# One new order for all the steps of a fused recurrence and MLP kernel

## The chip, the cores and the metric

The kernel runs on one core of a Trainium2 chip. A core has five engines that each work through a queue of their own in order: PE (TensorE, matrix products), DVE (VectorE), ACT (ScalarE), POOL (GpSimd) and SP (SyncE, which here only issues DMA transfers). An engine waits for another by a semaphore: the first instruction that needs a result stops its whole queue until the result is there. The metric is the time of one execution in microseconds (us).

## The reference

Two blocks follow each other. The first is a recurrence over 768 time steps, for 4 batches with 8 heads each, with a state of 40 by 40 numbers per head:

```python
    for t in range(S):
        kt, vt, rt = (k[:, :, t], v[:, :, t], r[:, :, t])
        wt, at, bt = (w[:, :, t], a[:, :, t], b[:, :, t])
        y[:, :, t] = np.einsum('bhd,bhde->bhe', rt, state)
        Sa = np.einsum('bhde,bhe->bhd', state, at)
        state_decay = state * wt[:, :, None, :] - np.einsum('bhd,bhe->bhde', Sa, bt)
        state = state_decay + np.einsum('bhd,bhe->bhde', vt, kt)
```

Its result, put together over heads to 3072 rows of 320, goes through an MLP: `h = x @ w_in` (320 to 2048), the exact GELU, and `g @ w_out` (2048 to 320). The inputs of the recurrence are float32, the two weights come as float64, and the result is float32.

## The kernel before

**Tiling.** Time is cut into 12 chunks of 64 steps. Inside a chunk the recurrence is written as matrix products with masks; it needs the inverse of a triangular matrix for each batch and head. Between chunks the 40 by 40 states are handed on. The MLP of a chunk starts when the chunk's y is there. So three things run side by side: the preparation of a chunk from its inputs, which needs no state; the part that hangs on the state; and the MLP of the chunk before.

**The steps.** Each piece of work is a small function, a step, and carries the number of its chunk: `mh.3.6` is the step mh of chunk 3 with argument 6. Those that matter here, in the order in which one chunk meets them:

- `tw`, `lt`, `pw`, `ew`, `en` (DVE and ACT): logarithms of the decays, their running sum (`pw`, line 717) and two exponentials. `ta`, `tb`, `tk`, `tv`, `tr` turn the inputs (DVE transposes), `sa`, `sn`, `kc`, `sb`, `sk` scale them.
- `nm` (PE) makes the triangular matrices, `nk` (DVE) masks them, `nd` (ACT) copies a part, `nx` (DVE, line 925) writes them into the tile Nb as POOL wants them. There is one Nb.
- `iz` and `ic` (POOL, line 955): the inversion, 31 steps of a product into tmp and a sum into W. Each needs the one before it.
- `wx` (DVE, line 931) takes W out into Tt, `tc_` (DVE, line 1066) transposes it, `jm` (PE, line 1070), `jc`, `km`, `kt0`, `kt1` put the inverses of the blocks together; `wa` and `wb` are copies by ACT for the same end.
- `am`, `vm`, `av`, `ym`, `xm`, `sm`, `pk`, `pb`, `cu` are products of PE for the chunk, with `ak`, `vk`, `sc`, `xc0`, `xc1`, `yc` as what DVE and ACT do to their results. `oa`, `od` (DVE), `oc`, `ot` (ACT, lines 1267 and 1271) and `tn` (DVE) make the next state; `om` and the transfers `ox` make the MLP's input.
- `mh.c.0` to `mh.c.7` (PE, line 1302): the first MLP product, in tiles of 64 by 128, two at a time; `ge` (ACT) is the GELU. The second product is done with seven smaller ones, `m1` to `m7` (PE), on sums `s1` to `s4` (DVE), and put together by `e1`, `e3` (ACT copies out of PSUM) and `e2`, `e4`, `e5`, `e6` (DVE sums). `so` and `sz` store the output.
- Steps with an L in front load; `ce`, `cs`, `cm`, `cv`, `cl`, `cn`, `cg` turn the weights from 64 bit to 32 bit at the start. `warm` steps are products without use that keep PE busy at the start.

**What sets the order.** All engines are scheduled by hand: one long list of step names, the function `order`, is performed from its first name to its last, and every engine's queue holds its instructions in that order. Waits follow from it. A step that reads a tile which an earlier step in the list writes waits for it, and a step that overwrites a tile waits for earlier readers.

**PSUM.** Products land in four banks of PSUM, which the steps borrow and give back (`take` and `drop`, from line 176). A bank can hold two results: `m5` and `m6` share one, `take`n by `m5` for two readers, `e3` and `e4`.

```python
    def product(c, name, n, l_, r_):
        po = bank(f"{name}{c}") if n else take(f"{name}{c}", 2 if name == "m56_" else 1)
        for f in range(NF // 2):
            nc.tensor.matmul(po[:, n, :DM // 2], l_[:, f], r_[:, f], start=f == 0, stop=f == NF // 2 - 1)
    def e3(c):
        nc.scalar.copy(c22, result(c, "m56_", 0))
        drop(f"m56_{c}")
```

Of the kernel before, what the change touches and what calls it, by code (L numbers as in the profile page):

```python
# [18 lines left out]
def order(chunks, first_seven):  # L19
    return """  # L20
        first_ones.1 Lw.1 stripes_set identity pads_extra.1 sums_mask Lw.0 pads_r.1 warm.4.20 upper_mask
        pads_extra.3 La.0 pads_a.1 warm.4.0 pads_VR.1 pads_VR.0 of_half_set Lb.0 bias_set warm.4.13 pads_r.0 lg.1
        first_ones.0 pads_w.0 pads_rows.0 warm.4.25 pads_extra.0 Lb.1 pads_rows.1 onward_set lg.0 pads_w.1 wT.1
        pads_a.0 pads_extra.2 La.1 wT.0 warm.4.2 ew.1 Lf.0.1.0 ta.0 Lf.1.1.0 cu.0 Lf.0.0.0 cu.1 ec.0 Lf.1.0.0
        ew.0 sb.0 tb.0 sa.0 Lk.0 warm.4.15 sn.0 ec.1 nm.0 sb.1 Lf.2.0.0 warm_set tb.1 nk.0 Lf5.0.0 ta.1 sn.1 qt
        parity_set iz.1 sa.1 qm.0 qi.0.p qi.1.v nm.1 qz.0 warm_first ce.1 Lf.3.0.0 nk.1 qb.0.0.v Lf.3.1.0 qc.0
        cs.1 qb.0.1.a nd.1 qm.1 sk.0.p ce.0 nx.1 Lr.0 cm.1 Tt_zero tk.0 cs.0 cn.1 ic.1.0.4 qc.1 Lf.2.1.0 cl.1
        cx.1 qz.1 kc.0 Lf5.0.1 qb.1.0.v qa.1 qb.1.1.a cm.0 cy.1 ic.1.4.8 qm.2 Lf.0.0.1 cv.0 ce.3 LV.0 warm.4.18
        qz.2 am.0 qb.2.0.v qa.2 cs.3 ic.1.8.12 tr.0 Lf.1.0.1 ce.2 ak.0 Lw.2 qb.2.1.a cs.2 qc.2 Lf.0.1.1 rc.0 qm.3
        Lk.1 ic.1.12.16 Lf.2.0.1 qa.3 qz.3 Lf5.1.1 tv.0 qb.3.0.v qb.3.1.a cm.3 cm.2 cv.3 qm.4 vc.0 ic.1.16.20  # L30
        vm.0 qa.4 ql warm.4.4 vk.0 lg.2 Lf.2.1.1 ce.5 cv.2 av.0 Lf.3.1.1 ic.1.20.24 qc.3 qx jm.0 sk.1.v warm.4.24
        cs.5 Lf.1.1.1 cm.5 cv.5 Lf5.1.0 jc.0 km.0 xc0.0 xc1.0 ic.1.24.28 ce.7 Ls.3 cu.2 kt1.0 Ls.4 cs.7 kt0.0
        cm.7 sm.0 ic.1.28.31 cv.7 LV.1 ec.2 pk.0 sc.0.0 Lr.1 ce.9 sc.0.1 tk.1 cs.9 Lb.2 pb.0 kc.1 cm.9 cv.9 ce.4
        La.2 tv.1 om.0.1 om.0.0 Ls.2 cs.4 cm.4 Lf.3.0.1 vc.1 tr.1 od.0.1 cv.4 ox.0.0 am.1 rc.1 unused.v wT.2 ce.6
        sb.2 warm.4.1 one_set od.0.0 wx.1 ew.2 ta.2 ox.0.1 tb.2 sa.2 vm.1 sn.2 cs.6 cl.6 cm.6 nm.2 vk.1 oc.0 cn.6
        mh.0.0 nk.2 ot.0.1 cg.6 ot.0.0 ak.1 Ls.1 nd.2 Ls.0 nx.2 mh.0.1 iz.2 ce.8 tn.0 LV.2 unused.a mh.0.2 wb.1
        cs.8 ic.2.0.4 Lk.2 cm.8 cv.8 ge.0.0 av.1 Ls.6 ce.11 ym.1 ce.10 cs.11 ic.2.4.8 Ls.5 mh.0.3 tc_.1 Lr.2
        cm.11 yc.1 sk.2.v xm.1 cs.10 Ls.7 ge.0.1 cm.10 tv.2 ic.2.8.12 Ls.9 xc1.1 cv.10 xc0.1 Ls.10 jm.1 vc.2
        cv.11 Ls.8 tr.2 ce.12 tk.2 Ls.11 mh.0.6 ce.13 cs.12 ic.2.12.16 La.3 cm.12 kc.2 cs.13 mh.0.7 wa.1.1 cm.13
        jc.1 cv.12 rc.2 am.2 vm.2 cv.13 ic.2.16.20 ce.14 pm.0.0 Ls.13 cl.14 cs.14 Ls.12 ce.15 cm.14 ak.2 Lw.3  # L40
        cn.14 cs.15 km.1 wa.1.0 cg.14 vk.2 pm.0.1 kt1.1 ta.3 kt0.1 Ls.15 cm.15 Ls.14 cv.15 ic.2.20.24 ce.16 Lbt.3
        sm.1 ge.0.3 cs.16 ce.17 mh.0.4 sc.1.0 Lwt.3 sc.1.1 cl.17 ic.2.24.28 cm.16 mh.0.5 cs.17 Lr.3 cm.17 lg.3
        cv.16 pk.1 cn.17 cg.17 pb.1 ge.0.2 oa.1.0 cu.3 Lk.3 oa.1.1 pm.0.3 ec.3 od.1.0 Lw.4 ic.2.28.31 od.1.1 oc.1
        tw.3 ot.1.0 om.1.1 sk.3.p ot.1.1 om.1.0 av.2 tn.1 ox.1.1 pc.0.1 lt.3 ym.2 wx.2 iz.3 pm.0.2 tc_.2 yc.2
        unused.r pw.3 so.0.1 ew.3 tb.3 ox.1.0 jm.2 wb.2 en.3 pc.0.0 xm.2 jc.2 sn.3 km.2 xc0.2 tr.3 mh.1.0 xc1.2
        La.4 sa.3 wa.2.1 kt1.2 wa.2.0 nm.3 kt0.2 so.0.0 sm.2 nk.3 Lkt.3 mh.1.1 nd.3 sc.2.0 nx.3 lg.4 Lv.3 pk.2
        sc.2.1 ic.3.0.4 pb.2 ge.1.0 tk.3 mh.1.6 ic.3.4.8 oa.2.0 Lr.4 ta.4 mh.1.7 ws.0 LV.3 ws.1 mh.1.4 ge.1.3
        Lbt.4 ic.3.8.12 tr.4 mh.1.5 oa.2.1 Lk.4 kc.3 mh.1.2 tv.3 od.2.0 Lwt.4 ic.3.12.16 mh.1.3 od.2.1 oc.2
        om.2.0 vm.3 Lb.3 ge.1.1 am.3 ge.1.2 vk.3 m1.1 ot.2.1 ic.3.16.20 s1.1 ot.2.0 om.2.1 m2.1 s2.1 ox.2.1 ak.3
        m5.1 e1.1 tn.2 ws.3 av.3 e3.1 ic.3.20.24 s3.1 Lkt.4 ym.3 e2.1 tw.4 m6.1 yc.3 s4.1 ox.2.0 m3.1 ws.2 lt.4  # L50
        tk.4 m7.1 ic.3.24.28 e4.1 LV.4 tb.4 m4.1 e5.1 Lr.5 ic.3.28.31 xm.3 e6.1 pw.4 so.1.1 mh.2.6 xc0.3 La.5
        wx.3 ew.4 tc_.3 cu.4 sb.3 jm.3 en.4 so.1.0 mh.2.7 wb.3 sn.4 Lv.4 wa.3.0 jc.3 xc1.3 wa.3.1 km.3 sa.4 ec.4
# [1414 lines left out]
```

## Time and profile before

| | |
|---|---|
| time, median of 3 runs | 637.75 us (637.71 to 638.87) |
| span of the profiled execution, first to last instruction | 638.6 us |
| PE busy | 621.4 us, 97% |
| DVE busy | 457.9 us, 72% |
| POOL busy | 380.3 us, 60% |
| ACT busy | 323.6 us, 51% |
| DMA, mean | 100 GB/s |

The profile gives the busy time of each engine, groups of equal instructions by source line (count, busy us, mean ns of one, and the idle time just ahead of them with what ended it), the waits, and the chain of work that ended last. The profiled execution's own time is not listed apart from its span; the span lies within the range of the three runs and 0.85 us above their median. Times in a timeline count from the span's start. A row of the windows gives the stretch, its length, then for PE, its weight loads (PEld), DVE, ACT and POOL the busy us and the number of instructions, then the granted clock of PE as a share of the full one, the share of DMA and its GB/s.

### The profile page before, as it was taken

To read this page: it belongs to the slowest core of one execution; us is meant where nothing else is said; L and a number is where in the kernel's file an instruction comes from. 1 tells how busy PE (TensorE), PEld (TensorE's weight loads), DVE (VectorE), ACT (ScalarE), POOL (GpSimd) and SP (SyncE) were. 2 spreads that over 40 slices of the span, in tenths; PEclk is the share of its full clock that TensorE was granted. 3 is DMA by queue.
4 is the path that set the end of the run, shared out by engine and by line. 5 is a ranking of instruction groups with operands and counts; after the bars stand their busy time and mean duration, and the time that the engine had idled before them with its cause. 6 is when DMAs were issued, how large, how long until landed. Compare 5 with 4: busy or idle time off the path is not lost.

```text
span 638.6 us, 27896 instructions
## 1 busy us (share of the span) xinstructions
PE 621.4 (97%) x12418; PEld 548.3 (86%) x12418; DVE 457.9 (72%) x557; ACT 323.6 (51%) x456; POOL 380.3 (60%) x782
## 2 busy tenths in 40 slices
...
GB/s 136 181 162 178 91 178 187 143 104 137 91 135 149 59 98 159 64 147 111 110 84 133 76 93 107 88 88 157 68 92 109 41 37 84 42 26 3 36 7 21
DMA packets 246899, 64.07 MB, mean 100 GB/s; under 512 B 228380, under 2 KB 243644, under 8 KB 246780
## 3 DMA queue, kind: packets, MB, share of 16 engines
...
## 4 chain that ended last, share of the span: by engine, by line
PE 76%; ACT 2%; DVE 0%; issue 0%; DVEq 0%
PE bank L1307 30%; PE bank L1346 27%; PE bank L193 19%; ACT Tt L937 0%; ACT SM L1154 0%; ACT L1312 0%; ACT spare L922 0%; DVE spare L864 0%; ACT st L1194 0%; ACT gt L1312 0%; ACT T L942 0%; DVE Tt L932 0%; ACT st L1192 0%; ACT Tt L1116 0%; DVE os L1299 0%
## 5 line engine op out<-in xcount | busy, mean ns | idle before, releaser
L1307 PE MATMUL bank<-xt,w_in_sb 64*128 64x256 f32 x1920 | 221.3, 381 | 0.2 <-ACT gt L1312 0.2
L961 POOL TENSOR_TENSOR tmp<-W,Nb 128x126 f32<-128x126 f32 (+22 forms) x341 | 164.4, 482 | 93.1 <-DVE Nb L927 67.6
L1307 PEld LDWEIGHTS bank<-xt,w_in_sb 64*128 64x128 f32 x1920 | 182.5, 187 | 25.1 <-issue 1.5
L963 POOL TENSOR_TENSOR W<-W,tmp 128x126 f32<-128x126 f32 (+22 forms) x341 | 168.8, 495 | 26.7
L1346 PE MATMUL bank<-w_out_sb,gt 128*128 128x160 f32 x704 | 101.1, 301 | 0.0
L1346 PEld LDWEIGHTS bank<-w_out_sb,gt 128*128 128x128 f32 x704 | 96.6, 190 | 2.2 <-issue 1.2
L1312 ACT ACTIVATE gt<-bank 128x1024 f32<-128x1024 f32 x48 | 48.7, 1024 | 94.9 <-PE bank L1307 94.6
L1175 DVE TENSOR_TENSOR SM<-bank,upper 128x832 f32<-128x832 f32 (+1 forms) x24 | 23.0, 988 | 20.3 <-PE bank L193 20.2
L1263 ACT COPY conv<-st 32x128 f32<-32x128 f32 (+2 forms) x55 | 28.0, 509 | 17.0 <-DVE st L1257 16.2
L1299 DVE TENSOR_TENSOR conv<-gt 128x1024 f32<-128x1024 f32 x11 | 14.2, 1290 | 25.1 <-ACT gt L1312 25.0
L1227 DVE TENSOR_TENSOR st<-bank,st 128x832 f32<-128x832 f32 (+1 forms) x22 | 21.2, 985 | 14.0 <-PE bank L193 14.0
L1346 PE MATMUL bank<-extra,conv 128*128 128x160 f32 x208 | 30.3, 300 | 0.0
L1299 DVE TENSOR_TENSOR os<-os,bank 128x160 f32<-128x160 f32 x44 | 13.8, 315 | 22.1 <-PE bank L1346 20.5
L1346 PEld LDWEIGHTS bank<-extra,conv 128*128 128x128 f32 x208 | 28.9, 190 | 0.1
L721 DVE TENSOR_TENSOR_SCAN kT<-spare,kT 128x256 f32<-128x256 f32 x36 | 26.6, 798 | 0.6 <-ACT kT L714 0.6
L1346 PE MATMUL bank<-extra,gt 128*128 128x160 f32 x176 | 25.8, 300 | 0.0
L1346 PEld LDWEIGHTS bank<-extra,gt 128*128 128x128 f32 x176 | 24.5, 190 | 0.1
L789 POOL TENSOR_TENSOR bk_rows<-bk_rows,part 128x640 f32<-128x640 f32 x9 | 14.3, 1591 | 14.3 <-ACT part L742 13.9
L1312 ACT ACT_TABLE_LOAD x17 | 21.8, 1283 | 0.3
L1346 PE MATMUL bank<-extra,SM 128*128 128x160 f32 x144 | 21.2, 300 | 0.0
L193 PEld LDWEIGHTS bank<-SM,Tt 64*64 64x64 f32 x768 | 17.1, 133 | 4.2 <-issue 2.3
L193 PE MATMUL bank<-SM,Tt 64*64 64x104 f32 (+1 forms) x768 | 19.3, 249 | 0.9 <-ACT Tt L1113 0.9
...
## 6 DMA issues: line engine op xcount, KB each, us to landing
...
```

The lines of the kernel that those rows point to most:

```text
L193: nc.tensor.matmul(o, lhsT, rhs, start=first, stop=True, skip_group_check=True)
L721: nc.vector.tensor_tensor_scan(logs[:, at:at + n], onward, logs[:, at:at + n], 0.0, ALU.mult, ALU.add)
L789: (nc.vector if q == "v" else nc.gpsimd).tensor_tensor(to, rows(k_of(c)), decays(c), ALU.mult)
L961: nc.gpsimd.tensor_tensor(t, W[:, BL // 2 - rows:, rest:rest + 1].to_broadcast([P, rows, rest]), Nb[:, rest:rest + 1, :rest].to_broadcast( ...
L963: nc.gpsimd.tensor_tensor(own, own, t, ALU.add)
L1175: nc.vector.tensor_tensor(SM[:, g, :, :, cols], pair_of(f"S{c}_", g).rearrange("p x i c -> p i x c")[:, :, :, cols], kept, ALU.mult)
L1227: nc.vector.tensor_tensor(to, pair_of(f"QY{c}_", g)[:, :, :, cols], to, ALU.add)
L1263: nc.scalar.copy(apart.rearrange("p e i g d -> p (e i g) d")[to_rows, :, to_col:to_col + n], st.rearrange("p e i g c -> p (e i g) c")[rows ...
L1299: nc.vector.tensor_tensor(to, one_, other, how)
L1307: nc.tensor.matmul(ph[:, x, s], w_in_sb[half(x), kt, p * P:(p + 1) * P], xt[half(x), kt], start=kt == 0, stop=kt == NK - 1)
L1312: nc.scalar.activation(gt[:, 4 * q:4 * q + 4].rearrange("p (x s) t -> p x s t", x=2), bank(f"ph{c}_{q}").rearrange("p x (s t) -> p x s t", ...
L1346: nc.tensor.matmul(po[:, n, :DM // 2], l_[:, f], r_[:, f], start=f == 0, stop=f == NF // 2 - 1)
```

## The change

The list in `order` is replaced by another list of the same 1450 steps. Every step is performed once, as before, with the same arguments; the functions are the same. The first MLP product stays in tiles of 64 by 128. What differs is the place of nearly every step, from the first memset to the last sums, so every engine's queue and SP's queue of transfers are in a new order, banks of PSUM are lent in a new order, and waits that follow from who comes first in the list are different ones. Below is the core of the diff: the two places from chunk 3 to chunk 5, and those around e3.6 and e3.9.

```diff
 def order(chunks, first_seven):
     return """
...
-        tk.4 m7.1 ic.3.24.28 e4.1 LV.4 tb.4 m4.1 e5.1 Lr.5 ic.3.28.31 xm.3 e6.1 pw.4 so.1.1 mh.2.6 xc0.3 La.5
-        wx.3 ew.4 tc_.3 cu.4 sb.3 jm.3 en.4 so.1.0 mh.2.7 wb.3 sn.4 Lv.4 wa.3.0 jc.3 xc1.3 wa.3.1 km.3 sa.4 ec.4
...
-        ak.4 pw.5 m3.2 e3.2 ew.5 m7.2 La.6 e2.2 ic.4.20.24 tn.3 en.5 e4.2 m4.2 e5.2 av.4 e6.2 tk.5 so.2.1
-        ic.4.24.28 ym.4 sn.5 Lr.6 mh.3.6 yc.4 sa.5 tv.5 LV.5 xm.4 ic.4.28.31 cu.5 xc1.4 xc0.4 mh.3.7 ec.5 wx.4
-        tc_.4 wa.4.1 iz.5 ta.6 nm.5 ge.3.3 vm.5 Lbt.6 tr.6 wb.4 jm.4 nk.5 mh.3.2 jc.4 nd.5 Lwt.6 wa.4.0 nx.5
...
-        s4.6 m5.6 so.5.0 oa.7.0 od.7.0 LV.9 om.7.0 m1.6 oa.7.1 ic.8.20.24 om.7.1 m2.6 s2.6 ox.7.1 od.7.1 ew.9
-        m6.6 s3.6 en.9 tr.9 ec.8 m3.6 e1.6 ic.8.24.28 oc.7 e2.6 sa.9 Lkt.9 e3.6 ot.7.0 m7.6 e4.6 ot.7.1 sn.9
...
-        ic.11.20.24 s3.9 m6.9 kc.11 od.10.0 m3.9 Lb.11 e3.9 e2.9 e4.9 ox.10.0 m7.9 ic.11.24.28 am.11 e5.9 vm.11
...
+        ta.4 m5.1 so.0.1 e3.1 s4.1 yc.3 ox.2.0 m6.1 ox.2.1 xm.3 xc0.3 xc1.3 e2.1 e4.1 m3.1 m7.1 wx.3 wa.3.0 m4.1 Lbt.4
+        tc_.3 jm.3 mh.2.4 Lv.4 wa.3.1 e5.1 mh.2.5 e6.1 lt.4 pw.4 Lkt.4 tb.4 mh.2.6 ew.4 so.1.1 sa.4 wb.3 en.4 mh.2.7
+        sn.4 jc.3 ge.2.2 km.3 tk.4 Lr.5 La.5 tv.4 nm.4 Lwt.5 ge.2.3 kt1.3 kt0.3 LV.4 nk.4 cu.4 Lw.5 nd.4 kc.4 so.1.0
+        sk.3.p iz.4 nx.4 ic.4.0.4 ic.4.4.8 ic.4.8.12 ic.4.12.16 sm.3 sc.3.1 mh.2.2 mh.2.3 sc.3.0 sb.3 ic.4.16.20
...
+        yc.4 lg.5 wx.4 wa.4.0 mh.3.6 tc_.4 jm.4 jc.4 tb.5 sn.5 xm.4 sb.4 tv.5 mh.3.7 so.2.1 ge.3.3 mh.3.2 xc1.4 Lkt.5
+        Lb.5 xc0.4 sa.5 nm.5 tk.5 cu.5 sk.4.p nk.5 kc.5 vm.5 Lwt.6 wa.4.1 wb.4 km.4 mh.3.3 ec.5 kt1.4 kt0.4 sm.4 vk.5
...
+        pk.7 pb.7 s2.6 oa.7.1 oa.7.0 LV.9 od.7.1 ec.8 od.7.0 om.7.0 oc.7 ot.7.0 ot.7.1 so.5.0 ic.8.20.24 ic.8.24.28
+        ic.8.28.31 om.7.1 ew.9 m1.6 m2.6 s3.6 Lv.9 Lb.8 tb.9 tn.7 ox.7.1 en.9 sn.9 sa.9 m5.6 e3.6 Lw.9 e1.6 e2.6 m6.6
...
+        e1.9 am.11 ak.11 ic.11.0.4 ic.11.4.8 ic.11.8.12 ic.11.12.16 s4.9 vk.11 od.10.1 oc.10 ot.10.1 ot.10.0 m5.9 e3.9
...
     """.split()
```

At the start the first transfers, too, are in a new order: before, Lw.1, Lw.0, La.0, Lb.0, Lb.1, La.1 and then the weights (Lf); after, Lw.0, Lw.1, Lb.0, La.0, Lb.1, then two steps of weights, and La.1 behind them.

More of the change, by code (lines that the diff above doesn't have):

```diff
@@ L20, in order @@
     return """
[L21 to L50, printed above, removed]
```

127 lines of the change are left out of this document (76 added, 51 removed).

## The prediction

> **What bounds the kernel now.** I read the page first, then the busy times by stretch, the waits, the chain that ended last, and the timeline of single engines.
>
> ```profile
> span 638.6 us, 27896 instructions
> PE 621.4 (97%) x12418; PEld 548.3 (86%) x12418; DVE 457.9 (72%) x557; ACT 323.6 (51%) x456; POOL 380.3 (60%) x782
> ```
>
> ```profile
> 120.00:140.00 20.00, 17.12 (x406) 12.89 (x400) 15.08 (x21) 16.94 (x24) 7.49 (x12) 1.00 0.46 89
> ```
>
> PE is busy for 621.4 of 638.6 us. What it loses, 17.2 us, lies almost wholly in the first 140 us; the stretch shown, with 2.9 us of it, is the last that loses much. From there the chain that ended last is PE behind PE. So no order can gain more than some 17 us, but one that makes PE wait loses each microsecond of it. The question is whether PE, in its new order, ever reaches a step before its input is there. The candidates are the loops that leave PE and come back. Four pieces of the chain give PE's prices:
>
> ```profile
> 184.46 2.36 PE bank L1307 x20
> 202.98 3.01 PE bank L193 x128
> 210.51 2.02 PE bank L193 x128
> 212.54 15.41 PE bank L1346 x112
> ```
>
> That is, in order: one mh 2.36, pk with pb 3.01 (1.5 each, and I take the same for xm, which has as many products), am with vm 2.02 (1.0 each, nm too), the seven products m1 to m7 15.41 (2.2 each).
>
> The loop with least room is POOL's. Each chunk's 31 inversion steps (ic, L961 and L963) are one serial run, and the next chunk's run can start only when DVE has made its Nb (nx, L927).
>
> ```profile
> 184.01 0.51 POOL L963 TENSOR_TENSOR W<-W,tmp 128x16 f32<-128x16 f32 x1
> 199.13 0.24 POOL L961 TENSOR_TENSOR tmp<-W,Nb 128x31 f32<-128x31 f32 x1 [4.83 <-DVE Nb L927]
> 234.92 0.23 POOL L963 TENSOR_TENSOR W<-W,tmp 128x16 f32<-128x16 f32 x1
> 243.13 1.06 POOL L961 TENSOR_TENSOR tmp<-W,Nb 128x31 f32<-128x31 f32 x1 [6.01 <-DVE Nb L927]
> 278.28 0.23 POOL L963 TENSOR_TENSOR W<-W,tmp 128x16 f32<-128x16 f32 x1
> ```
>
> ```profile
> 186.30 0.71 DVE L1067 STREAM_TRANSPOSE turned<-Tt 128x512 f32<-128x512 f32 x1
> ```
>
> ```profile
> 187.45 0.75 PE L193 MATMUL bank<-turned,spare 32*32 32x32 f32 x64
> 239.27 0.75 PE L193 MATMUL bank<-turned,N 32*32 32x32 f32 x64
> 288.61 0.75 PE L193 MATMUL bank<-turned,spare 32*32 32x32 f32 x64
> ```
>
> The run of chunk 3 ends at 184.52, that of chunk 4 lasts from 199.13 to 235.15 (36.0), that of chunk 5 from 243.13 to 278.51 (35.4). After a run DVE does wx and tc_, and PE's jm takes the result. tc_.3 ends at 187.01 and jm.3 starts at 187.45: there the loop has 0.44 us of room. Between two runs POOL has gaps of 14.6 and 8.0 us. PE needs 51.8 us from jm.3 to jm.4 and 49.3 to jm.5, without a pause.
>
> **The change, part by part.** No product, copy or transfer comes or goes. The order of instructions of the two built programs shows two things besides places: ACT's table loads go from 48 to 59, and PE's m6 now waits for e3 in chunks 1, 3, 5, 6, 7 and 9, where it did in 1, 8 and 10. m5 and m6 share a bank; where e3 (which copies m5's half out) is written ahead of m6, the program waits for it. Prices of the steps used below:
>
> ```profile
> L932 DVE STREAM_TRANSPOSE Tt<-W 128x512 f32<-128x512 f32 x11 | 7.6, 695 | 1.2 <-POOL W L963 1.2
> L942 ACT COPY T<-Tt 32x256 f32<-32x256 f32 x22 | 8.8, 402 | 18.1 <-DVE Tt L932 17.7
> L1299 DVE TENSOR_TENSOR os<-os,bank 128x160 f32<-128x160 f32 x44 | 13.8, 315 | 22.1 <-PE bank L1346 20.5 <-DVE os L1299 0.5
> L734 ACT ACT_TABLE_LOAD x7 | 9.0, 1283 | 6.7 <-DVE kT L721 6.6
> L734 ACT ACTIVATE wpT<-kT 128x512 f32<-128x512 f32 x18 | 10.6, 627 | 9.0 <-DVE st L1257 5.0 <-DVE xt L1233 3.9
> L738 ACT ACTIVATE kT<-kT 128x1024 f32<-128x1024 f32 x9 | 9.5, 1057 | 0.3
> L757 DVE STREAM_TRANSPOSE kT<-v_pairs 128x1024 f32<-128x1024 f32 x9 | 11.2, 1240 | 4.1 <-PE bank L193 4.1
> L922 ACT COPY spare<-spare 32x512 f32<-32x512 f32 x12 | 7.4, 616 | 9.5 <-DVE spare L864 9.4
> L784 DVE SCALAR_TENSOR_TENSOR bk_rows<-bk_rows,part 128x640 f32<-128x640 f32 x9 | 7.8, 867 | 0.6 <-DMA bk_rows<-in_b_dram 0.6
> L1312 ACT ACTIVATE gt<-bank 128x1024 f32<-128x1024 f32 x48 | 48.7, 1024 | 94.9 <-PE bank L1307 94.6
> L1299 DVE TENSOR_TENSOR conv<-gt 128x1024 f32<-128x1024 f32 x11 | 14.2, 1290 | 25.1 <-ACT gt L1312 25.0
> L1227 DVE TENSOR_TENSOR st<-bank,st 128x832 f32<-128x832 f32 (+1 forms) x22 | 21.2, 985 | 14.0 <-PE bank L193 14.0
> L1257 DVE TENSOR_TENSOR st<-st,wpT 128x320 f32<-128x320 f32 x20 | 13.8, 701 | 0.1
> L1263 ACT COPY conv<-st 32x128 f32<-32x128 f32 (+2 forms) x55 | 28.0, 509 | 17.0 <-DVE st L1257 16.2
> L1391 ACT COPY os<-bank 128x160 f32<-128x160 f32 x11 | 3.2, 295 | 27.5 <-PE bank L1346 26.2 <-DVE os L1299 1.3
> ```
>
> ```profile
> 183.15 2.52 DVE L721 TENSOR_TENSOR_SCAN kT<-spare,kT 128x256 f32<-128x256 f32 x4
> ```
>
> *Part 1, the inversion loop of chunks 3 to 5.* DVE does its queue in order, so what stands behind wx waits for POOL's run. Before, pw.4 stands ahead of wx.3, and sn.5, sa.5, tv.5, tk.5 and xc1.4 ahead of wx.4: they are done while POOL still inverts. In the new order wx.3 stands ahead of e5.1, e6.1 and pw.4, and wx.4 ahead of tb.5, sn.5, sb.4, tv.5, xc1.4, sa.5 and tk.5. This work now comes after the run and not beside it.
> Gap between the runs of chunks 3 and 4: wx 0.70, tc_ 0.71, the five small additions of e5 and e6 at 0.315 (1.58), pw 2.52, a table load 1.28, ew 2 x 0.627, wb 2 x 0.402, en 1.06, sn, tk and tv at 1.24 (3.72), kt1 0.70 (as wx), nk 1.24 (as the transposes, same size), nd 2 x 0.616, nx 1.24: 18.0 us. With a run of 36.0, jm.4 can follow jm.3 after 54.0. PE's own work between them: the 51.8 of before less xm.4 (1.5), nm.5 and vm.5 (1.0 each), which now come behind jm.4: 48.3. PE waits 5.7.
> Gap between chunks 4 and 5: wx 0.70, tc_ 0.71, seven passes of 1.24 (tb, sn, tv, sa, tk, nk, kc: 8.68), sb 0.87, xc1 0.98 (as L1227, same size), kt1 0.70, kt0 0.62, nd 1.23, nx 1.24: 15.7. With a run of 35.4: 51.1. PE's work: 49.3 less two mh (4.72), plus xm.4 1.5, nm.5 1.0 and cu.5 0.63 (the piece at 184.46 ends at 186.82, jm.3 starts at 187.45, with cu.4 between): 47.7. PE waits 3.4.
> At jm.3 itself the mh and the cu that stood ahead of it now stand behind: PE comes 3.0 earlier (187.45 - 184.46), has 0.44 of room, and waits 2.5. Behind jm.5 stands mh.4.6, whose bank is free only after e4.3, which DVE now does behind tc_.5, e2.3 and tv.6: 0.32 + 1.24 + 0.32 = 1.9 against jm's 0.7, so 1.2 more.
> Something is given back, for the runs get shorter. A POOL step beside a DVE pass with two SBUF inputs takes longer than alone; the same form stands here both ways, and the DVE pass it met:
>
> ```profile
> 180.57 0.33 POOL L961 TENSOR_TENSOR tmp<-W,Nb 128x70 f32<-128x70 f32 x1
> 230.86 1.19 POOL L961 TENSOR_TENSOR tmp<-W,Nb 128x70 f32<-128x70 f32 x1
> ```
>
> ```profile
> 230.50 1.36 DVE L776 TENSOR_TENSOR aT<-aT,wpT 128x1024 f32<-128x1024 f32 x1
> ```
>
> That is 0.86 for a pass. Out of the run of chunk 4 and into a gap go kc.4, sn.5 and sa.5 (2.6); out of chunk 5's kc.5 (0.9); out of chunk 3's pw.4, priced as one pass (0.9). Between nothing and 4.4 I take all of it, as the trace has this price. [...]
> Part 1: (2.5 - 0.9) + (5.7 - 2.6) + (3.4 - 0.9) + 1.2 = 8.4. I take the start of chunk 3's run as before, see the bounds.
>
> *Part 2, m6.6 behind e3.6.* ACT now has e3.6 behind oc.7, ot.7, ew.9 and en.9, and oc.7 needs DVE's od.7, which stands behind s1, s4 and s2 of chunk 6. From the end of mh.6.5: ge 1.02, three additions at 1.29 (3.87), oa 2 x 0.985, od 2 x 0.70, oc and ot five copies at 0.509 (2.55), ew 1.25, en 1.06, e3 0.30: 13.4. PE has pk, pb and m1, m2, m5 of chunk 6 meanwhile: 3.01 + 6.6 = 9.6. PE waits 3.8. Before, m6.6 stood ahead of e3.6 and waited for none of it.
>
> *Part 3, m6.9 behind e3.9.* The same, with e3.9 behind oc.10 and ot.10, and od.10.1 behind s2.9, s3.9, ak.11, s4.9 and vk.11. From pb.10 on: oa 0.985, od 0.70, s1 1.29, oa 0.985, om 2 x 0.70 (as od), s2, s3, s4 3.87, ak and vk 2 x 1.24, od 0.70, oc and ot 2.55, e3 0.30: 15.3. PE has m1, m2, m5 of chunk 9 (6.6) and vm, am (2.02): 8.6, and a last rest of pb, 0.2. PE waits 6.5.
>
> *Part 4, the clock.* What PE's idle time does to its clock shows in one place, where PE was busy for 1.08 of 2 us:
>
> ```profile
> 22.00:24.00 2.00, 1.08 (x104) 0.99 (x105) 1.97 (x4) 0.82 (x2) 1.53 (x3) 1.00 1.11 204
> 24.00:26.00 2.00, 0.70 (x32) 0.63 (x35) 1.99 (x2) 0.00 (x0) 1.89 (x2) 0.74 0.57 122
> 26.00:28.00 2.00, 2.00 (x65) 1.88 (x62) 1.06 (x3) 1.05 (x2) 2.00 (x2) 0.50 0.88 202
> 28.00:30.00 2.00, 2.00 (x3) 0.86 (x3) 1.97 (x4) 1.04 (x3) 0.48 (x1) 0.50 1.20 152
> 30.00:32.00 2.00, 2.00 (x4) 0.67 (x2) 1.73 (x4) 1.76 (x3) 0.30 (x1) 0.56 1.15 173
> ```
>
> The granted clock falls to 0.50 and costs 2 x (0.26 + 0.50 + 0.50 + 0.44) = 3.4 us of full-speed work. Later waits of before are too short to try it: the 2.9 us lost in 120 to 140 left it at 1.00. A wait of 3.8 to 6.5 us in one piece is emptier than the stretch at 22, so I charge 3.4 behind parts 2 and 3 each, where PE is the bound again: 6.8. Behind jm.4 a slow stretch would only eat the wait at jm.5, and behind jm.5 the wait is short: I charge none there. Bounds: 0, and three times 3.4.
> [...]
>
> *Other edits.* The eleven added table loads are 11 x 1.28 = 14.1 us of ACT, which is 51% busy: free, but for those in the sums. SP's and POOL's other moves are covered by the same waits; POOL's sk.3 and sk.4 move ahead of the next run, into its gaps. m6 behind e3 in chunks 1, 3, 5 and 7 is free or costs one short copy. The start-up order is new on every queue. It may gain the slow stretch at 24 us (3.4) and some of PE's early waits, or lose as much, since loads of chunk 1 now stand behind more weights: taken at 0, bounds -6 and +6.
>
> **Sum.** 8.4 + 3.8 + 6.5 + 6.8 = 25.5. The span is 638.6, so 664.1; the runs shown have a median of 637.75, 0.85 below that span, and on that scale I say 663.2.
>
> **The rivals.** (a) The clock stays up, or drops once: 656.4 to 659.8. For it: 120 to 140. Against: 24 to 30. (b) The two e3 waits don't bite, because ACT and DVE arrive earlier than the mean rows say: 637.75 + 8.4 = 646.2, with a clock drop after jm.5 649.6. Against: both sums begin at a PE step close by, so a late PE doesn't help them. (c) The other side: the new start. PE loses up to 17.2 us there and 3.4 more to the clock. If its new order saves most of that, chunk 3's run begins as much earlier, part 1 is gone, and against parts 2 to 4 (17.1) stands a gain of up to 20.6: 634.3 at best. It decides from a gain of 17.1 on, or 10.3 if the clock stays up. Against it: DVE has the same conversions to do first and is nearly full there (1.97 of 2 at 22, 1.99 at 24, 1.97 at 28). (d) The start loses 6, and the runs give nothing back (4.4): 673.6; with a third clock drop 677.0. For it: the weights ahead of chunk 1's rows.
>
> **How the numbers follow.** Forecast 0.50; (a) 0.16; (b) 0.12; (c) 0.05 for faster, with 0.01 for no change; (d) 0.16. Within 0.2% is about what a measurement of this kernel can tell from no change. Faster 0.05, same 0.01, slower 0.94. The range takes in (a), most of (b), and (d): 647 to 677; the forecast's own is 657 to 670.
>
> **What would show it.** After: PE idle in front of jm.3, jm.4 and jm.5 (waits of PE for DVE's tc_, L1063 of the new file), POOL gaps of about 18 and 16 us between the runs of chunks 3, 4 and 5 and a run of chunk 4 nearer 33 than 36, two waits of PE's second product for ACT's e3 of about 4 and 7 us, and clock rows at 0.50 behind them. ACT and DVE busy times stay within the added table loads. I am wrong if PE's busy share after 150 us stays at 100%, or if the start shifts chunk 3's run by more than 6 us.

## The result and the profile after

The changed kernel takes 669.87 us (median of 4 executions, 666.95 to 671.20) where the kernel before takes 638.31 (4 executions, 637.71 to 642.05). The ratio is 1.047, with a 95% interval of 1.0432 to 1.0508. The forecast was 663.2 us, 647 to 677.

The busy times on the page of the changed kernel, whose span is 668.8 us:

```profile
PE 629.3 (94%) x12418; PEld 556.0 (83%) x12418; DVE 457.9 (68%) x557; ACT 337.9 (51%) x467; POOL 374.8 (56%) x782
```

The span grew by 30.2 us. DVE is busy as long as before, ACT 14.3 us longer (the eleven table loads), POOL 5.5 shorter. PE's idle time went from 17.2 to 39.5 us, and PE's busy time rose by 7.9 although no product was added: most of it is work at half clock. So the two things that the prediction charged, waits of PE and falls of its clock, are the two things that show. Where they lie is told by the busy times by stretch of the changed kernel (columns as under "Time and profile before": stretch, length, PE busy, its weight loads, DVE, ACT, POOL, granted clock, DMA share, GB/s):

```profile
0.00:180.00 180.00, 164.47 (x3618) 132.36 (x3622) 142.81 (x183) 115.81 (x160) 115.24 (x233) 0.98 0.75 138
180.00:230.00 50.00, 48.33 (x854) 44.38 (x844) 38.22 (x46) 26.93 (x36) 30.29 (x68) 1.00 0.68 117
230.00:262.00 32.00, 27.94 (x715) 23.98 (x717) 20.60 (x25) 16.69 (x22) 11.46 (x34) 0.89 0.48 80
...
288.00:304.00 16.00, 12.75 (x168) 10.90 (x170) 8.10 (x14) 4.67 (x8) 10.33 (x29) 0.79 0.62 96
...
420.00:434.00 14.00, 10.60 (x78) 10.36 (x77) 12.81 (x15) 5.33 (x11) 12.35 (x22) 1.00 0.61 117
434.00:564.00 130.00, 128.55 (x2738) 116.09 (x2740) 87.09 (x102) 72.05 (x96) 75.17 (x169) 1.00 0.44 83
564.00:590.00 26.00, 19.78 (x254) 19.17 (x247) 16.05 (x20) 3.21 (x8) 18.88 (x35) 0.87 0.13 26
```

and of the kernel before:

```profile
0.00:180.00 180.00, 166.84 (x3599) 134.59 (x3600) 141.17 (x188) 118.64 (x161) 115.75 (x243) 0.98 0.76 143
180.00:638.60 458.60, 454.52 (x8822) 413.71 (x8820) 316.74 (x370) 204.99 (x295) 264.51 (x540) 1.00 0.45 84
```

Before, 4.1 us are lost after 180, 3.6 of them at the very end when PE is done. In the changed kernel PE loses time in seven places. Counting as lost the idle time of a stretch, and half of the time in which PE was busy at half clock:

| stretch of the changed kernel | what stands there | predicted | measured: idle + clock |
|---|---|---|---|
| 0 to 180 | start | 0 (-6 to +6) | 2.4 more than before |
| 180 to 230 | jm.3 (and sm.3) | 1.6 | 1.7 + 0 |
| 230 to 262 | jm.4 | 3.1 + 0 | 4.1 + 3.4 |
| 288 to 304 | jm.5, mh.4.6 | 3.7 + 0 | 3.3 + 3.0 |
| 420 to 434 | m6.6 | 3.8 + 3.4 | 3.4 + 0 |
| 434 to 564 | (nothing named) | 0 | 1.5 + 0 |
| 564 to 590 | m6.9 | 6.5 + 3.4 | 6.2 + 2.6 |

The measured column sums to 31.6, or 31.1 without the 0.5 that before loses between 180 and its end; the spans differ by 30.2, and the start holds products that nobody waits for, so its 2.4 is the least exact. Of the 4.1 us of idle time around jm.4, 2.8 are the wait itself and 1.3 a gap inside km.4, for which the profile shows no cause. PE's timeline shows the waits one by one:

```profile
188.04 0.75 PE L189 MATMUL bank<-turned,spare 32*32 32x32 f32 x64 [0.77 <-DVE turned L1063]
...
200.85 1.66 PE L189 MATMUL bank<-SM,Tt 64*64 64x104 f32 x64 [0.90 <-ACT Tt L1112]
...
239.64 0.86 PE L189 MATMUL bank<-turned,N 32*32 32x32 f32 x64 [2.77 <-DVE turned L1063]
...
295.01 1.08 PE L189 MATMUL bank<-turned,spare 32*32 32x32 f32 x64 [2.76 <-DVE turned L1063]
296.58 0.80 PE L1303 MATMUL bank<-xt,w_in_sb 64*128 64x256 f32 x2 [0.49 <-DVE os L1295]
...
429.58 1.63 PE L1342 MATMUL bank<-extra,SM 128*128 128x160 f32 x10 [3.40 <-ACT os L1387]
...
579.57 2.77 PE L1342 MATMUL bank<-extra,SM 128*128 128x160 f32 x9 [6.22 <-ACT os L1387]
```

These are jm.3, sm.3, jm.4, jm.5, mh.4.6, m6.6 and m6.9. All but sm.3, which waits for ACT's kt0.3, stand behind the step that the prediction named; jm.3 waits half of what was said, and sm.3 makes up for it. POOL's runs, too, come near to what was said, but one gap between them does not. The timeline of POOL at the end of the runs of chunks 3 and 4 and at the start of the next:

```profile
186.27 0.23 POOL L959 TENSOR_TENSOR W<-W,tmp 128x16 f32<-128x16 f32 x1
...
204.14 0.24 POOL L957 TENSOR_TENSOR tmp<-W,Nb 128x31 f32<-128x31 f32 x1 [15.18 <-DVE Nb L923]
...
237.70 0.23 POOL L959 TENSOR_TENSOR W<-W,tmp 128x16 f32<-128x16 f32 x1
...
258.57 0.24 POOL L957 TENSOR_TENSOR tmp<-W,Nb 128x31 f32<-128x31 f32 x1 [18.28 <-DVE Nb L923]
```

Gap 17.6 (18.0 said), run of chunk 4 from 204.14 to 237.93 = 33.8 (33.4 said), but the second gap is 20.6 and not 15.7.

### The profile page after: what moved, and what is told of

Its sections match the earlier page's. It is cut to its first block, busy times and chain, and to the rows that moved or that the text cites. A ratio compares the mean times of both kernels' runs of the same rounds, so it can differ in the third digit from the quotient of the medians.

```text
span 668.8 us, 27937 instructions
## 1 busy us (share of the span) xinstructions
PE 629.3 (94%) x12418; PEld 556.0 (83%) x12418; DVE 457.9 (68%) x557; ACT 337.9 (51%) x467; POOL 374.8 (56%) x782
## 4 chain that ended last, share of the span: by engine, by line
PE 53%; POOL 24%; SPq 6%; issue 6%; DVE 6%; ACT 3%; DMA 1%; POOLq 0%; DVEq 0%; ACTq 0%
PE bank L1303 23%; PE bank L1342 17%; PE bank L189 12%; POOL W L959 12%; POOL tmp L957 11%; SPq L443 2%; SPq L533 2%; SPq L1244 1%; DVE Nb L923 1%; ACT conv L1259 1%; POOL conv L654 1%; PE bank L1424 1%; DMA gt<-in_moe_w_in_dram 1%; DVE st L1223 1%; DMA xt<-xt 1%
## 5 line engine op out<-in xcount | busy, mean ns | idle before, releaser
L1303 PE MATMUL bank<-xt,w_in_sb 64*128 64x256 f32 x1920 | 225.6, 388 | 3.6 <-DMA xt<-xt 2.4
L957 POOL TENSOR_TENSOR tmp<-W,Nb 128x126 f32<-128x126 f32 (+22 forms) x341 | 162.4, 476 | 116.7 <-DVE Nb L923 91.0
L1303 PEld LDWEIGHTS bank<-xt,w_in_sb 64*128 64x128 f32 x1920 | 186.8, 191 | 30.6 <-issue 2.8
L959 POOL TENSOR_TENSOR W<-W,tmp 128x126 f32<-128x126 f32 (+22 forms) x341 | 164.2, 482 | 26.7
L1259 ACT COPY conv<-st 32x128 f32<-32x128 f32 (+2 forms) x55 | 28.0, 510 | 35.8 <-DVE st L1253 35.1
L1342 PE MATMUL bank<-extra,SM 128*128 128x160 f32 x144 | 23.7, 323 | 10.4 <-ACT os L1387 10.4
L1342 PEld LDWEIGHTS bank<-extra,SM 128*128 128x128 f32 x144 | 21.9, 206 | 11.4 <-ACT os L1387 11.3
L942 POOL MEMSET W<- 128x512 f32 x11 | 5.8, 524 | 35.8 <-DVE Tt L928 35.8
L1188 ACT COPY st<-bank 128x512 f32<-128x512 f32 x11 | 6.4, 584 | 36.5 <-PE bank L189 36.5
```

What stands on the lines that cost most here:

```text
L957: nc.gpsimd.tensor_tensor(t, W[:, BL // 2 - rows:, rest:rest + 1].to_broadcast([P, rows, rest]), Nb[:, rest:rest + 1, :rest].to_broadcast( ...
L959: nc.gpsimd.tensor_tensor(own, own, t, ALU.add)
L1259: nc.scalar.copy(apart.rearrange("p e i g d -> p (e i g) d")[to_rows, :, to_col:to_col + n], st.rearrange("p e i g c -> p (e i g) c")[rows ...
L1303: nc.tensor.matmul(ph[:, x, s], w_in_sb[half(x), kt, p * P:(p + 1) * P], xt[half(x), kt], start=kt == 0, stop=kt == NK - 1)
```

## The experiments

All are edits of the list of steps. In the order below they are called after_again, e3_late, loop4, both_back, before_e3, mh_ahead, warm_all, fill, fill_two, start_before, before_again and before_warm. Source lines in their profiles are shifted by up to five. They ran on four chips, on which the kernel before had medians of 641.71 (after_again to both_back), 640.69 (before_e3, mh_ahead, warm_all, before_warm), 639.67 (fill, start_before, before_again) and 641.01 us (fill_two). A ratio is to the kernel before on the same chip.

### The changed kernel again

> The changed kernel once more, nothing edited. In its first profile PE waited 2.8 us at jm.4, 2.8 at jm.5, 3.4 at m6.6 and 6.2 at m6.9, and the granted clock fell to 0.50 behind jm.4, jm.5 and m6.9 but not behind m6.6. All falls and rises there lie a multiple of 3.413 us apart, as if the clock were decided once in each stretch of a fixed grid. Theory A (the grid): the waits come again within some 0.5 us; a fall needs a wait that fills most of one stretch, so the 2.8 and 3.4 us waits may change places in this (which of them costs a fall depends on where the grid lies in this execution), and m6.9 always falls. Times of single executions then spread by one or two falls, 1.7 to 3.4 us each: 665 to 672. Theory B (the place decides: what PE does behind the wait): the same three falls in every profile, and single times within 1 us of each other.

Measured: 668.29 us (667.63 to 669.40), ratio 1.0428 (1.0377 to 1.0478). The waits were 2.76, 2.77, 3.41 and 6.22. The falls of the clock moved: one stretch of 3.41 us behind jm.4 (there were two), two behind jm.5 and m6.9, and a 10.2 us one in the start, where the first profile has two of 3.41. By the busy times by stretch that is a clock of 0.95 over 230 to 262 us (0.89 in the first profile), 0.79 over 285 to 301, 0.87 over 562 to 588, and 0.97 over the first 180 us (0.98). The falls and rises of the first profile lie multiples of 3.413 us apart (240.09, 246.91, 294.70, 301.53, 578.01, 584.83); the fall behind jm.4 of the second, at 241.48, lies 1.39 us behind one of these edges. So theory A, but less simply than I put it. The first profile, with the grid's own stretches as windows, around the waits at m6.6 and jm.4:

```profile
424.42:427.84 3.42, 1.75 (x13) 1.51 (x12) 3.42 (x5) 3.29 (x7) 3.10 (x5) 1.00 0.98 171
427.84:431.25 3.41, 1.67 (x12) 1.68 (x13) 3.41 (x4) 2.04 (x5) 2.94 (x7) 1.00 0.14 36
236.68:240.09 3.41, 0.64 (x54) 0.48 (x56) 2.02 (x3) 2.32 (x3) 3.03 (x9) 1.00 0.93 184
240.09:243.50 3.41, 3.41 (x98) 3.10 (x86) 3.38 (x4) 1.66 (x2) 0.20 (x2) 0.50 0.40 62
243.50:246.92 3.42, 3.42 (x16) 2.79 (x18) 3.42 (x4) 0.00 (x0) 0.00 (x0) 0.50 0.64 129
```

The wait of 3.40 us at m6.6 straddles an edge: either stretch still has PE busy for 1.7 of 3.41 us, and the clock stays up. The shorter wait of 2.77 us at jm.4 lies in one stretch, PE is busy for 0.64 us of it, and the next two stretches run at 0.50. The second profile adds a case in which idleness alone doesn't explain it (windows of the repeated run, before and behind the fall at 241.48):

```profile
238.07:241.48 3.41, 2.47 (x130) 2.33 (x132) 3.29 (x4) 2.27 (x3) 1.53 (x4) 1.00 0.85 140
241.48:244.89 3.41, 3.41 (x18) 2.78 (x18) 3.41 (x4) 0.00 (x0) 0.00 (x0) 0.50 0.18 36
```

PE is idle for 0.94 us only, but among its products are jm.4's 64 of 32x32, and the clock falls all the same.

### e3 behind m6

```diff
-m5.6 e3.6 Lw.9 e1.6 e2.6 m6.6 m4.6
+m5.6 Lw.9 e1.6 e2.6 m6.6 e3.6 m4.6
-m5.9 e3.9 m6.9 m3.9
+m5.9 m6.9 e3.9 m3.9
```

> The changed kernel with e3.6 behind m6.6 and e3.9 behind m6.9, nothing else moved. Theory A (parts 2 and 3 of the prediction): the two waits go, 3.4 and 6.2 us, and with m6.9 the fall of the clock behind it (PE stood 8.7 us further back after m6.9 than before it, so 2.5 of clock): 669.9 - 3.4 - 8.7 = 657.8. PE is busy throughout 420 to 430 and in the 20 us around m6.9. Rival B (the wait only moves on): PE then waits at m4, m3 or the next chunk's products for the same late ACT and DVE work, and at most half comes back: 664 or more. Rival C: a wait for e3 was not what held m6, time unchanged at 669.9.

Measured: 655.57 us (654.51 to 660.55), ratio 1.0243 (1.0180 to 1.0305); against the repeated changed kernel, which ran on the same chip, 12.7 us less. The stretches around m6.6 (422.3 here) and m6.9 (566.0):

```profile
412.00:426.00 14.00, 14.00 (x212) 13.51 (x208) 12.15 (x14) 8.10 (x14) 12.43 (x21) 1.00 0.70 134
556.00:576.00 20.00, 20.00 (x376) 19.46 (x372) 16.61 (x21) 3.22 (x8) 17.47 (x33) 1.00 0.17 34
```

PE doesn't pause, so nothing behind the two products was late: theory A, and B and C are out. In this order, parts 2 and 3 are the place of one short copy.

### The work of chunk 5 back beside the inversion

```diff
-Lbt.5 am.4 ... lg.5 wx.4 wa.4.0 mh.3.6 tc_.4 jm.4 jc.4 tb.5 sn.5 xm.4 sb.4 tv.5 mh.3.7 so.2.1 ge.3.3 mh.3.2 xc1.4
-Lkt.5 Lb.5 xc0.4 sa.5 nm.5 tk.5 cu.5 sk.4.p nk.5 kc.5 vm.5 ... vk.5 nd.5 iz.5 nx.5
+Lbt.5 Lkt.5 am.4 ... lg.5 tb.5 sn.5 tv.5 mh.3.6 xm.4 sa.5 tk.5 xc1.4 xc0.4 mh.3.7 wx.4 wa.4.0 tc_.4 nm.5 ge.3.3
+vm.5 jm.4 jc.4 nk.5 nd.5 sb.4 so.2.1 mh.3.2 Lb.5 cu.5 sk.4.p kc.5 ... vk.5 iz.5 nx.5
```

> The changed kernel with the second half of part 1 undone: tb.5, sn.5, tv.5, sa.5, tk.5 and xc1.4 (with xm.4, xc0.4, mh.3.6, mh.3.7 that they need or stand with) ahead of wx.4, and nm.5, vm.5 ahead of jm.4, about as before; Lkt.5 is issued earlier for tk.5. Theory A: the DVE work goes back beside POOL's run of chunk 4. The run of chunk 4 gets longer again (33.8 to 35.5 or 36), the POOL gap behind it falls from 20.7 to some 10 us, the wait of 2.8 us at jm.4 goes, and so does the fall of the clock behind it: PE stood 7.9 us further back at am.5 than at mh.3.6, and that comes back: 662.0. If POOL's earlier run of chunk 5 takes the wait at jm.5 with its fall too, 6.3 more: 655.7. Rival B (PE's own order and not DVE's place sets jm.4): the wait stands at nm.5 or mh.3.2 instead, and less than 3 us comes back: 667 or more.

Measured: 661.92 us (659.56 to 662.31), ratio 1.0314 (1.0253 to 1.0375), 6.4 less than the changed kernel on the same chip. No wait and no fall at jm.4 any more; jm.5 still waits 1.9, mh.4.6 0.8. In its profile the clock fell behind m6.6 (0.50 from 421.86 to 425.27), which neither profile of the changed kernel has; without that the gain of this execution would be nearer the 7.9 expected. POOL's timeline:

```profile
203.18 0.24 POOL L956 TENSOR_TENSOR tmp<-W,Nb 128x31 f32<-128x31 f32 x1 [15.18 <-DVE Nb L922]
...
233.97 1.41 POOL L958 TENSOR_TENSOR W<-W,tmp 128x70 f32<-128x70 f32 x1
...
236.54 1.13 POOL L958 TENSOR_TENSOR W<-W,tmp 128x45 f32<-128x45 f32 x1
...
238.70 0.23 POOL L958 TENSOR_TENSOR W<-W,tmp 128x16 f32<-128x16 f32 x1
...
250.42 0.24 POOL L956 TENSOR_TENSOR tmp<-W,Nb 128x31 f32<-128x31 f32 x1 [9.12 <-DVE Nb L922]
```

The run of chunk 4 is 35.8 us again (33.8 in the changed kernel), the gap behind it 11.5 (20.6). The step of 128x45 at 236.54 takes 1.13 us, and DVE's timeline has at 236.27 the pass sa.5 beside it (1.27 us); in the changed kernel that step stands alone, and so does the one of 128x70:

```profile
234.93 0.33 POOL L959 TENSOR_TENSOR W<-W,tmp 128x70 f32<-128x70 f32 x1
...
236.41 0.27 POOL L959 TENSOR_TENSOR W<-W,tmp 128x45 f32<-128x45 f32 x1
```

The difference is 0.86. The step of 128x70 meets the other pass that came back (sn.5, 233.96 to 235.19) and takes 1.08 longer. That is 1.94 for the two, and the run grew by 2.0.

### Both

The two edits together.

> Both edits together (e3_late and loop4). Theory A: the parts are independent, since they lie 170 us apart and PE is the bound between them: 669.9 - 12.1 - 7.9 = 649.9. What is then left over the kernel before, 638.3, is 11.6: the wait at jm.5 with its fall (6.3), some 2 at jm.3 and sm.3, 1.5 from the start, and small waits of some 2 behind 440. Rival B (one slack takes up both): the sum of the two gains is not reached by over 2 us, 652 or more.

Measured: 647.12 us (646.04 to 651.28), ratio 1.0108 (1.0049 to 1.0166), 21.2 less than the changed kernel on that chip, where the single gains of 12.7 and 6.4 sum to 19.1. The gains add up, within the spread of the executions; B falls. What is left over the kernel before on that chip, 5.4 us (3 to 11 by the interval), has jm.5 and mh.4.6 in it (1.65 and 0.81 us of wait).

### e3 ahead of m6 in the kernel before

```diff
-ew.9 m6.6 s3.6 en.9 tr.9 ec.8 m3.6 e1.6 ic.8.24.28 oc.7 e2.6 sa.9 Lkt.9 e3.6 ot.7.0 m7.6
+ew.9 oc.7 ot.7.0 e3.6 m6.6 s3.6 en.9 tr.9 ec.8 m3.6 e1.6 ic.8.24.28 e2.6 sa.9 Lkt.9 m7.6
-s3.9 m6.9 kc.11 od.10.0 m3.9 Lb.11 e3.9 e2.9 ... od.10.1 ... oc.10 ... ot.10.0 ... ot.10.1
+s3.9 od.10.0 od.10.1 oc.10 ot.10.0 ot.10.1 e3.9 m6.9 kc.11 m3.9 Lb.11 e2.9
```

> The kernel before with parts 2 and 3 alone: oc.7, ot.7.0 and e3.6 ahead of m6.6, and od.10.0, od.10.1, oc.10, ot.10.0, ot.10.1 and e3.9 ahead of m6.9. Theory A: the two waits come as in the changed kernel, some 3.4 and 6.2 us, with a fall of the clock behind m6.9 of 2.5 to 2.9 and by chance one behind m6.6: 12 to 14 us above the kernel before, ratio 1.019 to 1.022. Rival B (the waits belong to the new order around them, not to e3's place): under 6 us.

Measured: 649.63 us (649.06 to 653.34), ratio 1.0152 (1.0122 to 1.0182): 8.9 us over the kernel before. PE's waits in its profile:

```profile
PE bank L1341 <- ACT os L1386: 8.2, 2, 5.9
```

2.26 at m6.6 and 5.93 at m6.9, and a fall of two stretches behind m6.9. So the waits belong to e3's place behind oc and ot, which moved with it here, and come in the old order too. The time expected was too high by 3 to 5 us; 1.4 of it is in the two waits, and en.9, which stands ahead of e3.6 in the changed kernel, stands behind it here.

### Real work in the wait at jm.4

```diff
-mh.3.6 tc_.4 jm.4 jc.4 tb.5 sn.5 xm.4 sb.4 tv.5 mh.3.7
+mh.3.6 tc_.4 mh.3.7 jm.4 jc.4 tb.5 sn.5 xm.4 sb.4 tv.5
```

> The changed kernel with one product, mh.3.7 (2.4 us), ahead of jm.4, which waits 2.8 us there, so that real work fills the wait. Theory A (the loop of POOL and DVE sets the time there): jm.4's wait falls to some 0.4, but PE is at the next step that needs DVE's late work so much earlier, nm.5 behind sa.5, and waits there 2 to 3 us; the runs of POOL stay where they are, and the time is unchanged but for a fall of the clock more or less: 666 to 671. Theory B (PE's order alone made the wait): the wait and the fall behind it go, 2.4 and 3 to 5 us: 662 to 664.

Measured: 667.43 us (664.97 to 669.68), ratio 1.0417 (1.0386 to 1.0447), which can't be told from the changed kernel. PE's timeline at nm.5:

```profile
246.99 1.31 PE L188 MATMUL bank<-aT,nT 40*64 40x64 f32 x62 [1.60 <-DVE aT L771]
```

jm.4's wait went from 2.77 to 0.66 us, and nm.5 behind it waits 1.60 for DVE's sa.5; a fall of two stretches follows a little later, at 248.1 (0.83 over 240 to 260 us). That is theory A. Not as expected, jm.5's wait halved (2.76 to 1.44): the slow stretches last until 254.97, while km.4 is done at 252.5, and from there on a slow PE only eats into the wait at jm.5 (the section on the prediction takes this up).

### Useless products in the waits: the clock by itself

Three kernels put products of 128x512 that nobody reads in front of the waiting steps. The first uses the step warm, which borrows a bank for each product, the second and third one free bank that isn't borrowed:

```diff
-tc_.4 jm.4
+tc_.4 warm.4.4 warm.4.4 warm.4.4 jm.4
...
+    def fill(n):
+        at = idle[0]
+        for i in range(n):
+            mm(banks[at][:, 0], ident, cum_m.unsqueeze(1).to_broadcast([P, 4, P]))
```

> The changed kernel with products that nobody reads (the step warm, 128x512, some 0.86 us each at full clock) put into PE's four long waits: three ahead of jm.4, of jm.5 and of m6.6, seven ahead of m6.9. The waits stay as long as they are; only PE's clock is kept up. Theory A (part 4, the clock is a cost of its own): no fall to 0.50 behind any of the four, and what it cost there comes back. In the two profiles of the changed kernel PE lost 7.8 and 5.9 us from mh.3.6 to m1.3, 6.3 and 6.5 around jm.5, 9.1 and 9.2 around m6.9; less the waits of 2.8, 2.8 and 6.2 and 0.5 at mh.4.6 these are falls of 5.0 or 3.1, 3.0 or 3.2, and 2.9: some 10 in all, 669.1 - 10 = 659. Theory B (a slow stretch only eats into the next wait): at jm.5 PE comes earlier and waits longer, and only the fall behind m6.9 comes back: 666. Theory C (the falls are not set by PE's idleness): unchanged, 669.

Measured: 676.72 us (674.28 to 679.84), ratio 1.0565 (1.0533 to 1.0597): 6.9 and 8.4 us above the two medians of the changed kernel, on other chips. This one tells little of the clock, since the edit made waits of its own: the borrowed banks still had readers, so that a useless product ahead of jm.5 waited 3.5 us for DVE and one ahead of m6.6 2.1 us for ACT, and the clock fell behind both (jm.5 takes 0.94 us there and 0.75 in fill, and the clock is 0.96 over 400 to 440 us).

> As warm_all, but the useless products of one wait all go into one bank that is free, and the bank is not borrowed, so that they wait for no reader and the lending order stays: three ahead of jm.4, jm.5 and m6.6, six ahead of m6.9. In warm_all the second and third borrowed other banks and waited for their readers (3.5 us for DVE's e5 or e6 ahead of jm.5, 2.1 for ACT's e1 ahead of m6.6), which made new waits; the first place, where they did not wait, had PE lose 5.0 us with the useless products counted, against 7.8 and 5.9. Theory A (the clock is a cost of its own): no fall behind the four waits, PE reaches every wait's end as before: 669 less 1 to 3 (jm.4), 3 (jm.5) and 2.9 (m6.9), 660 to 662. Theory B (a slow stretch behind jm.4 or jm.5 only eats into the next wait): only the fall behind m6.9 comes back: 666. Theory C (the falls have another cause): 669.

Measured: 671.17 us (670.27 to 673.29), ratio 1.0488 (1.0446 to 1.0529). The clock stayed up around all four waits; here the stretch around m6.9 (useless products count as busy):

```profile
562.00:588.00 26.00, 24.92 (x359) 21.16 (x355) 17.06 (x22) 3.22 (x8) 19.42 (x36) 1.00 0.14 30
```

Locally that paid: POOL's gap behind chunk 4 is 18.2 us (20.6 and 18.8 in the two profiles of the changed kernel), and comparing PE's starts of the same steps it lost 2.9 to 3.1 us less around jm.5 and 2.6 less around m6.9. That is theory A at its places. But the execution as a whole was no shorter, as C would have it. PE's waits say where the rest went:

```profile
PE bank L188 <- issue: 6.9, 7, 2.0
...
PE bank L1308 <- issue: 1.2, 1, 1.2
```

"issue" are gaps in which PE waited for nothing that the profile shows; the changed kernel has 4.3 us of them in three gaps. Another gap of 1.5 us is at m1.8, which by the list needs oa.9.1, and that had ended 2.3 us earlier. A fall of the clock at 603.9 came on top, behind one of these gaps, and the time is 3.2 us above the span here; it is 1.9 to 2.7 in the other three executions of this kernel and 1.8 to 2.2 in those of all others. Why some 30 more products on PE bring gaps in places far from them was not settled.

> The useless products only where a fall of the clock came in every profile of the changed kernel and cost the same each time: three ahead of jm.5 and six ahead of m6.9. With all four places filled, the clock stayed at 1.00 there and PE lost 3.1 less around jm.5 and 2.6 less around m6.9, but it lost 3.5 more between m7.7 and jm.10 and about 3 more behind km.11, in gaps in which it waited for nothing that the program asks for, and the time was no better (671.2). Theory A (the falls at these two places cost 5.7, and those gaps came with the 42 added instructions or by chance): 669.1 - 5.7 = 663.4 if the gaps stay away. Rival B (what the clock gives back there is lost again further on, whatever the gaps are called): 668 to 671.

Measured: 666.33 us (663.82 to 666.86), ratio 1.0376 (1.0338 to 1.0413). No fall at jm.5 or m6.9, 2.4 to 2.6 us less lost at each, and the new gaps are gone (issue 4.0 in all). In its profile the wait at m6.6 brought a fall this time. The time lies between what A and B expected, and the interval overlaps that of the repeated changed kernel (1.0377 to 1.0478, on another chip). So the price of these falls is shown at its place in the traces; the whole time agrees with it but doesn't prove it.

### The start

The list begins with the first 383 steps of the list of before; all others follow in the order of the changed kernel.

> The first 383 steps in the order of before (up to wx.2, some 128 us), all others in the order of the changed kernel. PE had lost 14.0 us at jm.2 in the profile of before and 16.8 and 17.1 in the two of the changed kernel. Theory A (the start costs some 3 us, part of it falls of the clock that come by chance): 669.1 - 2.7 = 666.4, with the four long waits unchanged. Rival B (the start costs nothing, chunk 3's run starts when it did): 669. Rival C (the start is worth more, since the loop of chunks 3 to 5 begins with it): under 664.

Measured: 666.24 us (665.07 to 667.47), ratio 1.0405 (1.0372 to 1.0438); the four long waits are unchanged (2.76, 2.77, 3.41, 6.23). The median is that of theory A, 2.1 and 3.6 us below the two of the changed kernel, but on another chip, and the interval overlaps that of the repeated one. The traces put the start at somewhat less: POOL's run of chunk 3 begins at 147.38 us here, at 149.19 and 148.63 in the two profiles of the changed kernel, and at 146.82 and 147.27 in the two of the kernel before.

> The kernel before once more, for a second profile and the base on this chip: 638 to 642, PE waits of 1.4 at cu.3 and 1.5 at km.2 again, falls of the clock in the first 80 us alone, their number and length by chance.

Measured: 640.70 us (638.56 to 642.29), ratio 1.0008 (0.9988 to 1.0027). The waits came as expected, 1.45 and 1.53. The falls did not stay in the first 80 us: one came at 25.8, the other at 138.5, behind the wait at km.2.

The kernel before with useless products in its own waits:

```diff
-qm.0
+warm.2.4 warm.2.4 qm.0
...
-cu.3
+warm.4.4 cu.3
...
-km.2
+warm.4.4 km.2
```

> The kernel before with products that nobody reads in its three longest waits of PE: two of 128x256 ahead of qm.0 (wait 1.0 us at 21.3), one of 128x512 ahead of cu.3 (1.4 at 120.8) and one ahead of km.2 (1.5 at 136.7). Its single times went from 637.7 to 644.1 with mean clocks of 1.00 to 0.987, which is zero to five stretches of 3.4 us at half clock. Theory A (these three waits bring the falls): the clock stays nearer 1.00, and the median comes 1 to 4 us below that of the kernel before on the same chip, some 638. Rival B (the falls come from stretches of small products, where PE is busy but the array is not): nothing gained, ratio 0.998 to 1.003.

Measured: 641.33 us (638.19 to 643.46), ratio 1.0005 (0.9986 to 1.0024). Nothing gained, as rival B has it. In its profile the wait at cu.3 is gone, that at km.2 is down to 0.42 us, and one fall, at 27.6, remains. The mean clock did come out higher (0.997 in the median of its executions, 0.994 in that of the kernel before on the same chip), so these waits seem to have had a part in the falls; why the time did not follow was not settled. No version was found that beats the kernel before.

## Why the prediction came out as it did

The direction and the long waits were right, and the time is 6.7 us above the forecast, inside the range. That it is not further off is partly luck: falls of the clock that were charged and did not come (4.2 us) set off two thirds of those that came where none was charged (6.4). By the parts of the sum:

**Part 1, the inversion loop: right in its waits, wrong in what a slow PE does to it between chunks 4 and 5.** The first gap, the run of chunk 4 and the wait at jm.4 came near to what was said (17.6, 33.8 and 2.8 against 18.0, 33.4 and 3.1). What failed is the second gap: I added up DVE's work, 15.7 us, and it was 20.6. The chain of waits of the changed kernel shows another path (start, length, what):

```profile
239.64 3.84 PE bank L189 x113
243.48 6.23 PE bank L1303 x40
249.71 2.75 PE bank L189 x139
252.46 1.29 issue
253.75 0.74 PE bank L189 x49
...
257.18 1.26 DVE Nb L923
```

From tc_.4, which ends at 239.5, the chain goes to jm.4 and on through PE's queue (xm.4, mh.3.7, mh.3.2, nm.5, cu.5, vm.5, km.4) for 15 us; ACT's nd.5 stands behind kt0.4, which needs km.4, and DVE's nx.5 behind nd.5. In the prediction PE's work was only something that the loop had to outlast; here it is part of the loop. Five profiles with the same order at this place, but different falls of the clock, show how much of the 20.6 that is:

| profile | stretches at half clock from jm.4 to km.4 | gap of PE without a cause, just ahead of km.4 or in it | POOL's gap | POOL's gap without that |
|---|---|---|---|---|
| changed kernel | 2 | 1.29 | 20.6 | 19.3 |
| e3_late | 2 | 1.12 | 20.6 | 19.4 |
| after_again | 1 | 0.98 | 18.8 | 17.8 |
| start_before | 1 | 0.74 | 18.5 | 17.8 |
| fill | 0 | 1.97 | 18.2 | 16.2 |

In fill the useless products ahead of jm.4 are done when tc_.4 is, so they delay nothing here. Each stretch at half clock adds 1.6 us. At full clock 16.2 are left, near the 15.7 of DVE's sum. So DVE's work was added up well; the 4.9 us that were missing are 3.2 of slow clock and 1.3 of a gap, both of PE, and 0.5 of the rest.

The runs did get shorter, by 0.4, 2.2 and 0.5 us in chunks 3 to 5, together 3.1 where 4.4 was said. But 0.86 is not the price of a pass. The step of 128x45 in loop4 started 0.27 us into sa.5 and lost 0.86; that of 128x70 started together with sn.5 and lost 1.08. Both end 0.1 to 0.2 us behind the pass that they met, as the step of the prediction does (232.05 against 231.86). These three steps lost nearly what was left of the pass when they started: 0.86, 1.08 and 0.86 of 1.00, 1.22 and 1.00 us.

**Part 4, the clock: right that falls would cost several us, wrong in the places.** I charged 3.4 behind m6.6 and m6.9. They came behind jm.4 (3.4), jm.5 (3.0) and m6.9 (2.6): 9.0 where 6.8 was charged. The sentence that failed is "Behind jm.4 a slow stretch would only eat the wait at jm.5". Up to km.4 PE is in the loop, so a slow PE makes POOL's next run later, and jm.5 waits all the same: 2.76, 2.77 and 2.77 us in the three profiles of the table that have two or one slow stretches and none behind km.4. Its wait is set from the end of km.4 on (254.49 in the changed kernel): by nx.5 and POOL's run jm.5 can start 40.5 us later, and PE's own work until then takes 37.8. Behind km.4 the sentence holds: in e3_late a third slow stretch lies there, from 254.05 to 257.47, and jm.5 waits 0.67. And m6.6 brought no fall in the two profiles of the changed kernel, where its wait happened to straddle an edge of the grid and left PE idle for at most 1.89 us of a stretch. So in both the wait of 3.4 us kept the clock and the two of 2.8 us lost it (1.00 behind m6.6, 0.50 behind jm.4 and jm.5).

**Parts 2 and 3, the two e3 waits: right.** 3.4 and 6.2 us against 3.8 and 6.5, and taking e3 out of the way gave 12.7 us back, with the fall.

**Other edits: the start was not free.** Taken at 0, it made the run of chunk 3 begin 1.4 to 2.4 us later. This, the gap of 1.3 inside km.4 and 1.5 in small waits from 434 on are what else the sum lacked. And the 17.2 us that PE lost before don't lie "almost wholly" in the first 140 us: 13 do, and 3.6 lie at the very end, behind PE's last product. An order that only fills PE's waits could gain nearer 13 than 17, or 16 with the slow clock of the start.

**The scale.** I set the predicted span of 664.1 against the median by taking 0.85 off. In all runs here but fill the time is 1.8 to 2.2 us above the span of the same execution (670.69 against 668.8), so I estimate that the profiled execution of before took some 640.5 us, more than any of its three listed runs. Its later medians, 639.7 to 641.7, are nearer to it. With 1.9 added, the sum gives 666.0.

Of the rivals, (d) came nearest by its number, 673.6, but by wrong reasons: the runs did give back most of what was said, and the start lost some 2 us and not 6.
